# Regrouping a transposed activation in 4 KB rows: eight neighbouring feature blocks for each quarter of the partitions

## The chip, the cores and the metric

The kernel runs on one core of one Trainium2 chip. The metric is the device time of one execution in microseconds (us), as the median of repeated runs. Everything is float32.

## The reference

Two layers follow each other. The first is a global filter network: a real Fourier transform over the 3136 positions of each of 8 sequences, a product with a complex filter, and the inverse transform. The second is a feed-forward layer over the 25088 resulting rows, with 1024 hidden features:

```
X = rfft(x, axis=1);  y = irfft(X * (filt_r + 1j * filt_i))        # x: 8 x 3136 x 256
h = y.reshape(25088, 256) @ w_in                                    # 1024 features
solu = h * softmax(h)                                               # along the features
ln = (solu - mean(solu)) / sqrt(var(solu) + 1e-6) * g_ln
out = ln @ w_out                                                    # 1024 -> 256
```

## The kernel before

**Stages.** The Fourier transforms are written as matrix products with tables. A first stage (up to about 115 us) transforms sequence 0 alone and loads and converts the weights, which arrive as 64-bit words and are turned into float32 on VectorE, ScalarE and GpSimd (`load_words`, `load_float64`, `convert`). Then a loop over 196 steps `k` runs. One step handles 128 rows of the feed-forward layer; two steps make a pair `j`. Both matrix products of the layer use a seven-product scheme on a pair of row blocks, so operands have to be summed first: `pair_sums` for the first product (tiles `s`) and `project_sums` for the second (tiles `u`, and `solu_t` itself once), all on GpSimd through `sum_of` (L658). The transforms of sequences 1 to 7 are spread over the same steps by a table of step numbers (`PLAN`); they are done by about 1310 us.

**Order.** The order of all instructions on each engine is written out by hand in `step(k)`, under a manual schedule. Every engine runs its own queue in that order, and SyncE (SP) issues most transfers in that order too.

**The path of one block of rows.** `product` (L680, TensorE) makes `h` in PSUM; `keep` (L690, ScalarE) and `finish` (L701 and L704, VectorE) move it out and take the maximum; `exponential` (L712, ScalarE) and `normalize` (L723 to L728 on VectorE, L730 on ScalarE) give `solu` and its variance. The second product contracts over the features, so they have to come onto the partitions. `turn` (L738, VectorE) transposes 32 x 32 blocks of `solu` within each group of 32 partitions; four row blocks share one tile `turn`, laid out as [128 partitions, 32 feature blocks, 4 row blocks, 32]. `regroup` (L750) then moves the rest of the way by DMA, from SBUF to SBUF, on SP's queue: for each of two row groups of a pair it issues four transfers of 128 KB, one for each quarter `q` of the destination's partitions:

```
turned = turns[g].rearrange("p (k q) b i -> p k q (b i)", q=4)
for q in range(4):
    nc.sync.dma_start(out=st[32 * q:32 * q + 32, :, :],
                      in_=turned[32 * a:32 * a + 32, :, q, :])
```

Feature block `f` of 32 features is `f = 4 k + q` here: quarter `q` takes every fourth block, so a source row is eight separate pieces of 4 x 32 numbers, 512 B each, and the destination row is 4 KB in one piece. `solu_t` has two buffers for each row group, so a regrouping waits until the second product of two pairs before has read the buffer. After it, `project_sums` (L658, GpSimd) makes the sums, `project` (L792, TensorE) multiplies with `w_out_sb`, `keep_out` (L804, ScalarE) and `finish_out` (L809 and L811, VectorE) move the result out, and `store_out` (L819, SP) stores it. The small transfers `rows<-rs` (L758) and `rs_t<-rows` (L764) carry the reciprocal deviations from rows to partitions, on SP as well.

**The weights that follow this order.** `w_out_sb` and `g_sb` hold the features in the same order as `solu_t`. Four pieces of `w_out` (two halves of the features by two halves of the outputs) are each loaded by one GpSimd-issued transfer of 512 KB (L369), `(k p) d w -> p k d w`; `g_sb` comes by one transfer of single numbers (L536).

Of the kernel before, what the change touches and what calls it, by code (L numbers as in the profile page):

```python
# [17 lines left out]
P = 128  # L18
# [12 lines left out]
KD, KF = C // P, DFF // P  # L31
# [61 lines left out]
def kernel(  # L93
# [10 lines left out]
    nc = tc.nc  # L104
# [26 lines left out]
    g_sb = consts.tile([P, KF], FP32, name="g_sb")  # L131
# [11 lines left out]
    def words(ap):  # L143
        rows, cols = ap.shape
        return bass.AP(tensor=bass.DRamTensorHandle(ap.tensor.name, (2 * rows * cols,), I32),
                       offset=0, ap=[[2 * cols, rows], [2, cols], [1, 2]])

    w_in_words, w_out_words = words(moe_w_in), words(moe_w_out)
# [211 lines left out]
    with ExitStack() as st:  # L360
# [5 lines left out]

        def load_words(src, n):
            raw = wpool.tile([P, 512, 2], I32, name=f"raw_{n}", tag="raw")
            nc.gpsimd.dma_start(  # L369
                out=raw.rearrange("p (k d) w -> p k d w", d=src.shape[-2]) if len(src.shape) == 4 else raw,  # L370
                in_=src)
            return raw

        def load_float64(dst, raw, negate, share):
# [62 lines left out]
        for h in range(2):  # L437
            for half in range(2):
                weights.append((w_out_sb[:, (0, 6, 1, 2)[2 * h + half]].rearrange("p k d -> p (k d)"),
                                w_out_words[512 * h:512 * h + 512, P * half:P * half + P].rearrange(  # L440
                                    "(k p) d w -> p k d w", p=P)))

        def resident(held):
            def find(sp, u):
# [8 lines left out]
        def begin(j):  # L453
            raws[j] = load_words(weights[j][1], j)
# [35 lines left out]
        def idle(out):  # L490

            nc.tensor.matmul(out=out, lhsT=tables[0][0][:, 0, 0].rearrange("p u q -> p (u q)"),
                             rhs=filters[0][0][:, 0], start=True, stop=True)
# [13 lines left out]
        def start(i):  # L507
            sp.fetch_filter(i)
            sp.fetch_de(i)
            sp.forward(i, halves(f"pb_0_{i}"))  # L510
# [4 lines left out]
        for n in range(16):  # L515
            (nc.sync, nc.scalar)[n % 2].dma_start(
                out=t2_0[NH * (n % 4):NH * (n % 4) + NH, n // 4, :], in_=rows_x[n:n + 1])
# [6 lines left out]
        for i in range(units):  # L524
            if i + 2 < units:
                start(i + 2)
            sp.multiply(i, 0, nc.vector.tensor_tensor)
            sp.multiply(i, 1, nc.gpsimd.tensor_tensor)
            pss = [ps_t.tile([P, 2, C], FP32, name=f"pc_0_{i}_{u}", tag="t") for u in range(2)]
            idle(pss[0])  # L530
            sp.inverse(i, pss)
            sp.store(i, nc.scalar.dma_start)
            if i == 0:
                nc.gpsimd.dma_start(out=wi_t, in_=wi_dram)
                nc.gpsimd.dma_start(out=wq_t, in_=wq_dram)
                nc.gpsimd.dma_start(out=g_sb, in_=moe_g_ln.rearrange("(k p) -> p k", p=P))  # L536
            elif i != 2:
                begin({1: 2, 3: 3, 4: 4, 5: 5, 6: 6}[i])
        idle_row(14, "idler")
# [6 lines left out]
        for i0, n, rows in ((0, 4, P), (4, 4, P), (8, NP - 9, P), (NP - 1, 1, NQ)):  # L546
            f, at = filters[i0]
            nc.sync.dma_start(
                out=f_dram[i0:i0 + n].rearrange("i u q k c -> (u q) i (k c)")[0:rows],
                in_=f[0:rows, at:at + n].rearrange("p i k c -> p i (k c)"))  # L550
# [85 lines left out]
    def load_de(sp, u):  # L636
# [6 lines left out]
    turns, variances, solu_ts, solu_sums, rs_rows, rss, pos, ots = (  # L643
        {} for _ in range(8))
# [96 lines left out]
    def regroup(p, i):  # L741


        g, second = divmod(p, 2)
        turned = turns[g].rearrange("p (k q) b i -> p k q (b i)", q=4)
        a = 2 * second + i
        st = upool.tile([P, KF, P], FP32, name=f"solu_t_{p}_{i}", tag=f"solu_t{i}")
        solu_ts[p, i] = st[:, 0:KF // 2, :], st[:, KF // 2:KF, :]
        for q in range(4):
            nc.sync.dma_start(out=st[32 * q:32 * q + 32, :, :],  # L750
                              in_=turned[32 * a:32 * a + 32, :, q, :])
        if not second and i == 0:
            rs = small.tile([P, 4], FP32, name=f"rs_{g}", tag="rs", bufs=2)
            nc.gpsimd.tensor_scalar(out=rs, in0=variances.pop(g), scalar1=1.0 / DFF, scalar2=EPS_LN,
                                    op0=ALU.mult, op1=ALU.add)
            nc.gpsimd.tensor_tensor(out=rs, in0=rs, in1=neg_half, op=ALU.pow)
            rs_rows[g] = rows = rs_dram.tile([P, 4], FP32, name=f"rows_{g}", tag="rows")
            nc.sync.dma_start(out=rows, in_=rs)  # L758
# [137 lines left out]
    def step(k):  # L896
# [24 lines left out]
        if not odd and 0 <= j - 3 < pairs:  # L921
            regroup(j - 3, 0)
# [13 lines left out]
        if not odd:  # L936
            if hid:
                product(j, 6)
                keep(j, k + 1, 0)
            if proj:  # L940
                project(p, 3)
                project(p, 4)
            if 0 <= j - 3 < pairs:
                regroup(j - 3, 1)
            if 0 <= j - 4 < pairs:
                project_sums(j - 4, 1)
            if hid:
                product(j, 7)
        else:
            if proj:  # L950
                project(p, 1)
                keep_out(p, 0, (0, 0))
                project(p, 2)
                finish_out(p, 0, 0, (0, 0), 1)
            if hid:
                product(j, 3)
                product(j, 4)
            if 0 <= j - 3 < pairs:
                project_sums(j - 3, 0)
                if (j - 3) % 2 == 0:  # L960
                    regroup_deviations((j - 3) // 2)
            if proj:
                project(p, 6)
                project(p, 7)
# [52 lines left out]
```

## Time and profile before

| | |
|---|---|
| median of 6 runs | 1684.87 us (1677.85 to 1687.3) |
| the profiled execution | 1686.34 us, span 1684.6 us |
| granted TensorE clock, mean of the span | 0.986 |
| TensorE (PE) busy | 1602.5 us, 95% |
| VectorE (DVE), GpSimd (POOL), ScalarE (ACT) busy | 75%, 67%, 56% |
| bytes moved by DMA | 311.72 MB in 375957 packets |
| SP's queue (q1) | 306260 packets, 169.81 MB, 38.6% of the time of 16 DMA engines |
| `solu_t<-turn` (L750) | 784 transfers of 128 KB |

The page of the profile names engines as in the table; PEld is the loading of weights into TensorE, which overlaps the products, and SPq is SP's queue. A group of instructions is written as line, engine, operation, output tile `<-` input tiles, shape, count, then busy time and the mean of one, then the idle time of the engine just before these instructions and who ended it. Matrix products are pipelined and their ends are modelled, so a TensorE that is shown as busy need not run at its peak. All windows are in us from the start of the span.

### The profile page before, as it was taken

How to read it: one execution, taken by the hardware profiler on the slowest of the kernel's cores; microseconds unless marked ns; L12 is line 12 of the kernel's file. 1: busy time of each engine (PE TensorE's matmuls, PEld its weight loads, DVE VectorE, ACT ScalarE, POOL GpSimd, SP SyncE). 2: the span in 40 equal slices, each digit the busy share in tenths (PEclk: the TensorE clock that was granted, in tenths of full speed). 3: DMA queues.
4: the chain of work that ended last, by engine and by line, in shares of the span. 5: the costliest groups of instructions: out<-in, count | busy, mean ns of one | idle time of the engine just before them, and what ended most of it. 6: DMA issues, size and time to landing. Idle time of an engine off the chain costs nothing.

```text
span 1684.6 us, 31072 instructions
## 1 busy us (share of the span) xinstructions
PE 1602.5 (95%) x10022; PEld 1096.5 (65%) x10022; DVE 1265.9 (75%) x2619; ACT 937.9 (56%) x1730; POOL 1125.6 (67%) x1268
## 2 busy tenths in 40 slices
PE   5798899999999999999999999999999999999996
PEld 1353456756766676667766676667776777777776
DVE  1676787777778878887778878787778776777772
ACT  2154455556665555556565665556565566656551
POOL 4444777578666756687577866677566756676664
PEclk8998899999999999999999999999999999999999
DMA  9886868876788668865786658766775444444443
GB/s 260 248 276 208 238 182 230 215 200 181 195 240 226 179 180 232 222 188 149 210 241 197 176 152 234 226 183 167 200 210 166 114 124 123 100 108 107 110 110 94
DMA packets 375957, 311.72 MB, mean 185 GB/s; under 512 B 61514, under 2 KB 341571, under 8 KB 375795
## 3 DMA queue, kind: packets, MB, share of 16 engines
q1 hardware_dynamic: 306260, 169.81, 38.6%
q0 software_dynamic: 32640, 101.65, 20.2%
q10 hardware_dynamic: 36896, 38.28, 8.0%
q8 instruction: 81, 1.33, 0.3%
q14 instruction: 80, 0.66, 0.1%
HBM read 124.83 MB, written 81.50 MB: 122 GB/s over the span
## 4 chain that ended last, share of the span: by engine, by line
PE 65%; DMA 15%; DVE 8%; POOL 4%; issue 3%; SPq 3%; ACT 2%; ACTq 0%; DVEq 0%; POOLq 0%
PE m L680 27%; PE o L792 25%; DMA solu_t<-turn 7%; PE py L353 5%; SPq L750 2%; DMA x<-in_x_dram 2%; PE pb L292 2%; PE pc L292 2%; PE pa L260 2%; DVE h L728 2%; PE pa L217 2%; DMA t<-d 1%; DVE turn L738 1%; DMA rows<-rs 1%; DMA out_dram<-ot 1%
## 5 line engine op out<-in xcount | busy, mean ns | idle before, releaser
L730 ACT ACTIVATE e<-h,nmu 128x1024 f32<-128x1024 f32 x196 | 225.3, 1149 | 365.4 <-DVE h L728 363.5
L792 PEld LDWEIGHTS o<-w_out_sb,solu_t 128*128 128x128 f32 x3136 | 381.0, 192 | 61.0 <-issue 40.7
L792 PE MATMUL o<-w_out_sb,solu_t 128*128 128x128 f32 x3136 | 401.2, 276 | 12.1 <-DVE rsum L723 9.0
L680 PE MATMUL m<-w_in_sb,s 128*128 128x512 f32 x784 | 401.8, 604 | 4.3 <-ACT h L690 2.2
L792 PEld LDWEIGHTS o<-w_out_sb,u 128*128 128x128 f32 x2352 | 305.3, 192 | 146.9 <-issue 110.8
L658 POOL TENSOR_TENSOR u<-solu_t 128x512 f32<-128x512 f32 x98 | 146.1, 1491 | 307.1 <-DMA solu_t<-turn 178.1
L680 PE MATMUL m<-w_in_sb,y 128*128 128x512 f32 x588 | 316.0, 621 | 13.7 <-DVE nmax L704 10.5
L792 PE MATMUL o<-w_out_sb,u 128*128 128x128 f32 x2352 | 313.4, 276 | 6.3 <-ACT ot L804 4.6
L728 DVE SCALAR_TENSOR_TENSOR h<-e,rsum,h 128x1024 f32<-128x1024 f32 x196 | 292.2, 1491 | 6.9
L811 DVE SCALAR_TENSOR_TENSOR ot<-o,rs_t,ot 128x128 f32<-128x128 f32 x294 | 102.5, 348 | 204.7 <-ACT ot L804 168.7
L690 ACT COPY h<-m 128x512 f32<-128x512 f32 x294 | 173.7, 591 | 130.4 <-PE m L680 113.9
L738 DVE STREAM_TRANSPOSE turn<-h 128x1024 f32<-128x1024 f32 x196 | 242.3, 1236 | 0.8
L712 ACT ACTIVATE e<-h,nmax 128x1024 f32<-128x1024 f32 x196 | 226.3, 1155 | 0.0
L658 POOL TENSOR_TENSOR u<-solu_t,u 128x512 f32<-128x512 f32 x98 | 143.0, 1459 | 87.9 <-PE o L792 83.9
L704 DVE CUSTOM_DVE_ANT_0 h<-m,h 128x512 f32<-128x512 f32 x196 | 133.1, 679 | 83.4 <-ACT h L690 59.7
L680 PEld LDWEIGHTS m<-w_in_sb,y 128*128 128x128 f32 x588 | 95.7, 193 | 123.3 <-DVE nmax L704 64.6
L356 ACT COPY y<-py 128x392 f32<-128x392 f32 x128 | 109.5, 855 | 106.4 <-PE py L353 104.7
L353 PEld LDWEIGHTS py<-wi_t,t 100*128 100x128 f32 x1024 | 132.3, 192 | 54.0 <-issue 40.2
L680 PEld LDWEIGHTS m<-w_in_sb,s 128*128 128x128 f32 x784 | 123.9, 191 | 65.8 <-issue 45.6
L658 POOL TENSOR_TENSOR solu_t<-solu_t,solu_t 128x512 f32<-128x512 f32 x98 | 152.0, 1551 | 7.7
L658 POOL TENSOR_TENSOR u<-u,solu_t 128x512 f32<-128x512 f32 x98 | 136.9, 1397 | 0.7
L353 PE MATMUL py<-wi_t,t 100*128 100x98 f32 x1024 | 131.6, 273 | 0.8 <-DMA t<-d 0.4
(108 smaller groups left out, 1984.4 us busy)
## 6 DMA issues: line engine op xcount, KB each, us to landing
solu_t<-turn SPq DMA_DIRECT2D x784, 128.0 KB
out_dram<-ot SPq DMA_DIRECT2D x196, 128.0 KB
t<-d POOLq DMA_DIRECT2D x56, 400.0 KB, 4.9
d<-x POOLq DMA_DIRECT2D x100, 200.0 KB, 5.2
f<-f_dram POOLq DMA_DIRECT2D x39, 512.0 KB, 6.7
d<-g POOLq DMA_DIRECT2D x39, 512.0 KB, 5.1
t<-d ACTq DMA_DIRECT2D x36, 512.0 KB
x<-in_x_dram SPq DMA_DIRECT2D x112, 98.0 KB
```

Source lines behind the costliest of these rows:

```text
L353: nc.tensor.matmul(out=psv[:, i:2 * NCH - i:2 * NCH - 1 - 2 * i, :], lhsT=t4s[e, ch][:, i, cb * P:cb * P + P], rhs=wi_t, start=True, stop= ...
L356: evac(out=y[:, cb, t0:t0 + S].rearrange("p (r m j) -> p m j r", m=N2 // NCH, j=NCH)[:, ch:last + 1 - ch:last - 2 * ch], in_=psv.rearrange ...
L658: nc.gpsimd.tensor_tensor(out=out, in0=in0, in1=in1, op=op)
L680: nc.tensor.matmul(out=ms[j, bank], lhsT=lhsT, rhs=w_in_sb[:, w, :], start=m in (1, 2, 7), stop=True, skip_group_check=True)
L690: nc.scalar.copy(out=h_half(k, i), in_=ms[j, 0])
L704: nc.vector.tensor_tensor_reduce(out=h_half(k, i), in0=ms[j, bank], in1=h_half(*kept), scale=1.0, scalar=sofar, op0=ALU.add, op1=ALU.min, ...
L712: nc.scalar.activation(out=e, in_=hs[k], func=AFT.Exp, bias=nmaxs.pop(k)[:, 1:2], scale=-1.0, accum_out=esum)
L728: nc.vector.scalar_tensor_tensor(out=solu, in0=e, scalar=rsum, in1=solu, op0=ALU.mult, op1=ALU.mult, accum_out=nmu)
L730: nc.scalar.activation(out=e, in_=solu, func=AFT.Square, bias=nmu, scale=-float(DFF), accum_out=variances[g][:, i:i + 1])
L738: nc.vector.transpose(out=turns[g][:, :, i, :], in_=solus.pop(k).rearrange("p (f j) -> p f j", j=32))
L792: nc.tensor.matmul(out=pos[p, bank], lhsT=lhs[:, f, :], rhs=w[:, f, :], start=f == 0 and m in (1, 2, 7), stop=True, skip_group_check=True)
L811: nc.vector.scalar_tensor_tensor(out=ot, in0=pos[p, bank], scalar=rs, in1=out_half(p, *kept)[0], op0=ALU.mult, op1=ALU.add)
```

## The change

The order of the features on the partitions changes. Feature block `f` becomes `f = 8 q + k`: quarter `q` takes eight neighbouring blocks. A source row of a regrouping is then 8 x 4 x 32 numbers in one piece, 4 KB, like the destination row. The number of transfers (784), their size (128 KB) and their partitions stay. `w_out_sb` and `g_sb` are loaded in the new order; as the 128 partitions no longer follow from one regular step in memory, each of the four pieces of `w_out` and `g_sb` is loaded by four transfers of 32 partitions instead of one of 128. The order of instructions on the engines is otherwise the same: on GpSimd 15 more transfers are issued in the first stage, and no other instruction moves.

```
         def load_words(src, n):
             raw = wpool.tile([P, 512, 2], I32, name=f"raw_{n}", tag="raw")
-            nc.gpsimd.dma_start(
-                out=raw.rearrange("p (k d) w -> p k d w", d=src.shape[-2]) if len(src.shape) == 4 else raw,
-                in_=src)
+            if len(src.shape) == 3:
+                nc.gpsimd.dma_start(out=raw, in_=src)
+            else:
+                for q in range(4):
+                    nc.gpsimd.dma_start(
+                        out=raw[32 * q:32 * q + 32].rearrange("p (k d) w -> p k d w", k=KF // 2),
+                        in_=src[q])
             return raw
...
                 weights.append((w_out_sb[:, (0, 6, 1, 2)[2 * h + half]].rearrange("p k d -> p (k d)"),
-                                w_out_words[512 * h:512 * h + 512, P * half:P * half + P].rearrange(
-                                    "(k p) d w -> p k d w", p=P)))
+                                w_out_words.rearrange("(q h k p) d w -> h q p k d w", q=4, h=2, p=32)[
+                                    h, :, :, :, P * half:P * half + P]))
...
-                nc.gpsimd.dma_start(out=g_sb, in_=moe_g_ln.rearrange("(k p) -> p k", p=P))
+                for q in range(4):
+                    nc.gpsimd.dma_start(out=g_sb[32 * q:32 * q + 32],
+                                        in_=moe_g_ln.rearrange("(q k p) -> q p k", q=4, p=32)[q])
...
-        turned = turns[g].rearrange("p (k q) b i -> p k q (b i)", q=4)
+        turned = turns[g].rearrange("p (q k) b i -> p q k (b i)", q=4)
...
             nc.sync.dma_start(out=st[32 * q:32 * q + 32, :, :],
-                              in_=turned[32 * a:32 * a + 32, :, q, :])
+                              in_=turned[32 * a:32 * a + 32, q])
```

## The prediction

> **What bounds the kernel now.** I read the busy table and the slices first, then the DMA queues, then the stages, then who waits for whom, and the end last.
>
> ```profile
> PE 1602.5 (95%) x10022; PEld 1096.5 (65%) x10022; DVE 1265.9 (75%) x2619; ACT 937.9 (56%) x1730; POOL 1125.6 (67%) x1268
> PE   5798899999999999999999999999999999999996
> DMA  9886868876788668865786658766775444444443
> q1 hardware_dynamic: 306260, 169.81, 38.6%
> q0 software_dynamic: 32640, 101.65, 20.2%
> ```
>
> TensorE is busy in nearly every slice after the fifth; DMA is heavily used until about 1310 us and half as much after it. The change works on DMA, in SP's queue q1. So the question is how much of TensorE's remaining idle time hangs on those transfers. Busy time by stage (the transforms of sequences 1 to 7 end near 1310):
>
> ```profile
> core 0: us, PE busy (x) PEld busy (x) DVE busy (x) ACT busy (x) POOL busy (x), PEclk, DMA share, GB/s
> 168.00:210.00 42.00, 35.11 (x192) 16.49 (x191) 32.23 (x57) 18.91 (x36) 32.30 (x35) 0.88 0.80 236
> 210.00:1310.00 1100.00, 1078.20 (x7089) 748.54 (x7088) 875.83 (x1792) 649.30 (x1215) 774.40 (x879) 1.00 0.72 199
> 1310.00:1640.00 330.00, 328.22 (x1919) 241.35 (x1917) 249.08 (x562) 201.26 (x373) 220.45 (x235) 1.00 0.45 113
> 1640.00:1684.60 44.60, 30.79 (x241) 29.05 (x240) 13.07 (x29) 9.41 (x21) 19.37 (x16) 0.95 0.37 97
> ```
>
> From 210 to 1310 TensorE is idle for 1100 - 1078.2 = 21.8 us, from 1310 to 1640 for 1.8 us, and at the end for 13.8 us. These small numbers cap the change. Who waits, from 210 to 1310:
>
> ```profile
> POOL u L658 <- DMA solu_t<-turn: 155.5, 38, 7.7
> ...
> PE o L792 <- DVE rsum L723: 7.6, 20, 1.8
> PE m L680 <- DVE nmax L704: 7.0, 12, 1.1
> PE pa L260 <- POOL x L251: 3.9, 3, 1.6
> PE m L680 <- DVE h L701: 0.7, 3, 0.3
> ```
>
> GpSimd waits 155.5 us, 4.1 us at a time, for the regrouped tile. TensorE waits for VectorE (7.6 + 7.0 + 0.7 = 15.3 us) and a little for GpSimd (3.9 us), and hardly for a DMA. The chain of waits gives `solu_t<-turn` 7% of the span, but at two of its places that I looked at (517 and 553 us) the instruction named as released, L811, had stood in a VectorE queue with no idle time ahead of it. I take the 7% as no measure of a gain.
>
> **Part 1, the data movement.** 784 transfers of 256 pieces are 200,704 packets of 512 B; in the trace's packet records they take 32 ns each on the mean, which is 200,704 x 32 / 16 = 401 us for each of the 16 engines, 23.8% of the span. The change makes 784 x 32 = 25,088 packets of 4096 B. No SBUF to SBUF packet of that size is in the trace. The nearest rows are 4096 B packets of other transfers: 159 ns (median on q0 and q10), 218 ns (mean on q0 from 210 to 1310) and 241 ns (mean of the 1510 on q1, most of them in the crowded first stage). That bounds the new time at 249 to 378 us; I take 200 ns between the undisturbed and the crowded rows, 314 us, 18.6% of the span. DMA is relieved by about 5 points of its 72%.
>
> The rows of sizes give 512 B in 32 ns, 1024 B in 46 and 4096 B in 159, so 16, 22 and 26 bytes per ns: here small pieces between SBUF and SBUF do cost. The Trainium skill speaks against this change: "DMA: Bandwidth & Descriptors", section "Why small descriptors are slow (HBM only)", says that SBUF to SBUF transfers do not suffer the penalty of small descriptors. By that rule the packets would take as long as before in total, this term would be zero, and the sum would shrink to what the issue and the end give.
>
> **Part 2, the issue on SP.** L750 is 622 ns at the median, and 0.77 us on the mean from 168 to 1310 (425.5 us for 552). `rs_t<-rows` (L764) also goes to 32 partitions, each in one piece, and takes 424 ns (302 at least). I expect about 0.42 us, bounds 0.30 to 0.62. Four issues then save 4 x 0.2 = 0.8 us before the last of a group leaves.
>
> **Part 3, when GpSimd gets the tile.** Counting 256 packets to a transfer, the last packet ends 2.0 us after the issue from 1310 on, and 3.5 us (median; 6 at the ninth tenth) before it. A transfer's own share of an engine falls from 16 x 32 = 512 ns to 2 x 200 = 400 ns. With the issue (0.8), this (0.1) and, in the crowded stage, a shorter queue in front (1 us, two thirds of the 1.5 us by which the crowded landing exceeds the quiet one), a wait of 4.1 us shrinks by about 1.9 us: 38 x 1.9 = 72 of 155.5 us, 46%. That is GpSimd time, and most of it is covered: the sums made from the tile are read by TensorE one to two steps (6 to 12 us) later.
>
> **Part 4, what of it reaches TensorE between 210 and 1310.** Two ways are visible. First the direct wait for the sum L251, which stands behind the waiting sums in GpSimd's queue: 46% of 3.9 is 1.8 us (bounds 0 to 3.9). Second the meeting of GpSimd with VectorE:
>
> ```profile
> L728 DVE SCALAR_TENSOR_TENSOR h<-e,rsum,h 128x1024 f32<-128x1024 f32 x135 | 204.6, 1516 | 4.7
> ...
> L728 DVE SCALAR_TENSOR_TENSOR h<-e,rsum,h 128x1024 f32<-128x1024 f32 x51 | 71.1, 1395 | 1.8
> ```
>
> The first row is 210 to 1310, the second 1310 to 1640, where the tile lands early: L728 takes 1516 against 1395 ns; its shortest is 1283. It is longer where a GpSimd sum runs at the same time. VectorE's excess over 1283 is 135 x 0.233 = 31.5 us in the first stage, and TensorE's 15.3 us of waiting for VectorE make 0.49 us of each. If earlier landing brings L728 half way to the later stage's mean, 135 x 0.060 x 0.49 = 4.0 us are gained. Bounds: 15.4 us gained if all excess went; the loss is priced in the second rival. Part 4 is 5.8 us.
>
> From 168 to 210 I take nothing: TensorE's longest wait there (3.0 us) is for GpSimd's L315, behind a GpSimd queue that never waits for `solu_t`. From 1310 to 1640 nothing either, 1.8 us at most.
>
> **Part 5, the end.** After the last row block nothing covers the regrouping:
>
> ```profile
> 1660.92 6.31 SPq L750 DMA_DIRECT2D solu_t<-turn  x8
> 1669.18 1.27 POOL L658 TENSOR_TENSOR u<-solu_t 128x512 f32<-128x512 f32 x1 [4.66 <-DMA solu_t<-turn]
> 1673.15 1.13 PE L792 MATMUL o<-w_out_sb,u 128*128 128x128 f32 x8 [1.65 <-POOL u L658]
> ```
>
> Eight issues, the landing, three sums, then TensorE, which has waited 1.65 us. Eight faster issues (1.6 us) and 0.1 to 0.3 us of landing bring all of this forward by 1.7 us or more; then TensorE's own queue is next, so 1.65 us is the whole gain. If the issue stays at 0.62 us, 0.1 to 0.3 us is left.
>
> **Part 6, the extra loads.** GpSimd's issue of one `w_out` piece (512 runs of 1 KB) takes 0.78 us, of a `w_in` piece (128 runs) 0.58, of `g_sb` 0.93. Four of 128 runs each are 4 x 0.58 = 2.3, so 1.5 us more for each piece; `g_sb` becomes 4 x 0.6 = 2.4, likewise 1.5 more.
>
> - Behind `g_sb` stands the sum L315 of unit 1 (starts at 56.94): it would end near 59.7, and TensorE reads it at 63.97. Covered by 4 us.
> - Behind the `w_out` pieces at 73.49 and 76.65 stand the sums of units 5 and 6. The last one would start at 79.3 instead of 77.79 and end at 80.0, where TensorE wanted it at 79.56: TensorE and its row of idle products move by 0.5 us. At the price of 0.78 an issue it would be 1.4 us.
> - That shift meets a pause of 1.93 us at 117.5, where TensorE waits for a GpSimd sum that follows VectorE's conversions; these run without a gap from 77.6 to 112. So it costs nothing, and 0.5 to 1.4 us if that pause were not there.
> - The conversions need the pieces 8 us or more after they land, so the later landing is hidden.
>
> **The sum.** 0 + 5.8 + 0 + 1.65 = 7.4 us. Against the profiled execution, 1686.3 - 7.4 = 1678.9; that run is 1.5 us above the median of six, so against the median 1684.87 - 7.4 = 1677.5 us, 0.44% faster. What a measurement of this kernel can tell from no change is about 0.3%, 5 us. The forecast's own range is 1664 (all excess of L728, all 3.9 us and 1.65 gone: 21 us) to 1681.
>
> **Rivals.** First, the waits are covered: GpSimd's 155.5 us lie beside a busy TensorE, VectorE stays where it is, and only the end gains: 1684.9 - 1.65 = 1683.2. For it speak TensorE's 98% from 210 on and the absence of direct waits for DMA. Against it, the idle time is concentrated in the stage with crowded DMA.
>
> Second, slower: GpSimd takes the tile sooner and then holds up VectorE. The sum `u<-solu_t` has a median of 2.09 us from 1310 on and 1.27 before, so in the quiet stage it is GpSimd that loses 0.81 us to VectorE. If it starts 1.9 us sooner it can be ahead of L728, and VectorE loses this instead. With half of the 68 pairs between 210 and 1310, 34 x 0.81 x 0.49 = 13.5 us, minus the end: 1684.9 + 13.5 - 1.65 = 1696.7. It outweighs the other gains (1.65 + 1.8) once L728's mean there rises by 3.45 / 0.49 / 135 = 0.05 us, above 1.57 us. The same may come from L315 and L245, which meet GpSimd too.
>
> Third, the change does not do what it says: rows of 4 KB are cut to 512 B again, the packet count stays near 376 thousand, and the time stays at 1685.
>
> **Chances.** Forecast 0.50 (0.43 faster, 0.07 same); covered 0.24 (0.05, 0.16, and 0.03 slower); GpSimd ahead of VectorE 0.22 (0.02 same, 0.20 slower); rows cut 0.04 (0.03 same, 0.01 slower). That makes faster 0.48, same 0.28, slower 0.24. The range takes in the first rival and most of the second, 1664 to 1695.
>
> **What would show it.** Right: about 200 thousand packets, those of 4096 B on q1 at 160 to 240 ns; DMA share near 0.66 from 210 to 1310 and near 0.38 from there to 1640; L750 near 0.42 us; GpSimd's wait for `solu_t` near 85 us in that stage; L728 at 1.40 to 1.50 us; no wait of TensorE for `u` at the end. Wrong: L728 above 1.57 us, L750 still at 0.62, or GpSimd's waits gone while TensorE's idle time stays near 22 us.

## The result and the profile after

The changed kernel takes 1692.96 us, median of 24 runs (1684.81 to 1699.62), beside 1685.23 us for the kernel before, median of 48 runs (1677.82 to 1692.36). The ratio is 1.0044, 95% interval [1.0033, 1.0056]: 7.7 us slower, where 7.4 us faster was forecast. The profiled execution of the changed kernel took 1689.39 us, span 1687.6. Lines have moved by 6: the softmax product L728 is now L734, the sums L658 are L664, the regrouping L750 is L756.

From the page of the changed kernel, the busy table, the slices and the two large queues (packets, MB, share of 16 engines):

```profile
PE 1605.2 (95%) x10022; PEld 1098.4 (65%) x10022; DVE 1268.5 (75%) x2619; ACT 937.5 (56%) x1730; POOL 1127.9 (67%) x1283
...
PE   5898899999999999999999999999999999999997
...
DMA  9986868776788668766776668766785455444443
...
q1 hardware_dynamic: 130644, 169.81, 38.8%
q0 software_dynamic: 32928, 101.65, 20.1%
```

The pieces were joined: q1 has 175,616 packets fewer, 200,704 of 512 B having become 25,088 of 4096 B. The third column of q1 did not fall with them: 38.6% before, 38.8% now. Busy time by stage, changed kernel:

```profile
core 0: us, PE busy (x) PEld busy (x) DVE busy (x) ACT busy (x) POOL busy (x), PEclk, DMA share, GB/s
...
168.00:210.00 42.00, 34.43 (x194) 16.24 (x191) 31.38 (x56) 18.62 (x35) 32.03 (x35) 0.88 0.81 238
210.00:1310.00 1100.00, 1081.37 (x7120) 753.17 (x7118) 872.40 (x1801) 650.83 (x1218) 773.49 (x882) 1.00 0.72 199
1310.00:1640.00 330.00, 324.44 (x1871) 235.96 (x1870) 251.75 (x549) 198.16 (x366) 213.65 (x230) 1.00 0.46 110
1640.00:1687.60 47.60, 33.11 (x260) 31.19 (x259) 16.67 (x36) 10.89 (x24) 21.81 (x17) 0.95 0.40 98
```

DMA share stands where it was in every stage. TensorE's idle time shrank by 3.2 us from 210 to 1310 (to 18.6) and grew by 3.8 from 1310 to 1640 (to 5.6), in the stage where the forecast expected nothing. A second view of the same thing, counted from the trace's own records: the 196 transposes of VectorE (L738, now L744) mark the steps of the layer. From transpose 0 to 136 the kernel before takes 1120.8 us and the changed one 1115.0; from 136 to 144, 55.5 and 57.4; from 144 to 195, 328.9 and **337.0**. So the last stage lost 8.1 us, about the whole difference of the medians. The spans of these two executions differ by 3.0 us only (1684.6 and 1687.6), since the 5.8 us that the transform stage was shorter in this pair, and 1.2 us at the end, stand against it.

The waits of the changed kernel, 210 to 1310 (total us, times, longest), then the softmax product, first from 210 to 1310 and then from 1310 to 1640 (busy us, mean ns of one, idle before):

```profile
POOL u L664 <- DMA solu_t<-turn: 144.4, 36, 7.8
...
PE m L686 <- DVE nmax L710: 6.6, 11, 1.5
PE o L798 <- DVE rsum L729: 6.4, 22, 1.7
...
PE m L686 <- DVE h L707: 1.9, 4, 0.9
PE pa L260 <- POOL x L251: 1.8, 2, 1.1
```

```profile
L734 DVE SCALAR_TENSOR_TENSOR h<-e,rsum,h 128x1024 f32<-128x1024 f32 x136 | 202.3, 1487 | 4.8
...
L734 DVE SCALAR_TENSOR_TENSOR h<-e,rsum,h 128x1024 f32<-128x1024 f32 x50 | 78.5, 1570 | 1.8
```

GpSimd still waits 144 us for the tile (155.5 before), TensorE for VectorE 14.9 us (15.3 before) and for GpSimd's L251 1.8 (3.9 before). The product became a little shorter in the first stage (1516 before) and longer in the second (1395 before). There TensorE now waits for the VectorE operation that follows the product, from 1310 to 1640, before and after:

```profile
PE m L680 <- DVE h L701: 1.4, 3, 0.5
```

```profile
PE m L686 <- DVE h L707: 5.6, 14, 0.5
```

One place in the last stage shows how. Timeline of the kernel before (start, duration, instruction):

```profile
1550.11 1.28 DVE L728 SCALAR_TENSOR_TENSOR h<-e,rsum,h 128x1024 f32<-128x1024 f32 x1
1550.18 2.34 POOL L658 TENSOR_TENSOR u<-solu_t 128x512 f32<-128x512 f32 x1 [1.84 <-DMA out_dram<-ot]
...
1551.32 0.75 DVE L701 TENSOR_SCALAR_CACHE_REDUCE h<-m,nmax 128x512 f32<-128x512 f32 x1
```

And the same step of the changed kernel:

```profile
1549.19 1.26 POOL L664 TENSOR_TENSOR u<-solu_t 128x512 f32<-128x512 f32 x1 [1.66 <-DMA out_dram<-ot]
...
1549.31 2.23 DVE L734 SCALAR_TENSOR_TENSOR h<-e,rsum,h 128x1024 f32<-128x1024 f32 x1
...
1550.54 2.14 POOL L664 TENSOR_TENSOR solu_t<-solu_t,solu_t 128x512 f32<-128x512 f32 x1
...
1551.47 0.74 DVE L707 TENSOR_SCALAR_CACHE_REDUCE h<-m,nmax 128x512 f32<-128x512 f32 x1
...
1552.27 1.12 PE L686 MATMUL m<-w_in_sb,y 128*128 128x512 f32 x2 [0.38 <-DVE h L707]
```

At both places the one that starts first runs at its own speed (1.28 or 1.26 us), and the other takes about 1 us more (2.34 or 2.23 us). Before, VectorE starts 70 ns ahead here and GpSimd loses. After, GpSimd starts 0.12 us ahead, L734 takes 2.23 us, and TensorE stands 0.38 us for what VectorE does next. Over the 14 odd steps from 168 on, GpSimd's first sum starts 84 ns *after* L728 in the median before, with L728 at 1369 ns on the mean, and 84 ns *before* L734 after, with L734 at 2060 ns. The profile puts the sum's wait down to `out_dram<-ot`, but the sum follows its own tile: in these 14 steps it starts 0.37 to 0.56 us after the last packet of its regrouping before, and 0.39 to 0.61 us after it in the changed kernel. So an earlier tile is an earlier sum.

The page "SBUF — State Buffer" of the Trainium skill, section "SBUF: two separate sides", describes a port pair that VectorE and GpSimd share as an exclusive lock, held for a whole instruction by the one that starts first, the other blocking fully. The two timelines agree with it to about 0.2 us: by such a lock the second one would take its own time and what is left of the first one's, 2.47 and 2.42 us as an estimate from the rows above, where 2.34 and 2.23 were measured.

The end of the changed kernel, timeline:

```profile
1665.07 5.34 SPq L756 DMA_DIRECT2D solu_t<-turn  x8
...
1674.92 1.27 POOL L664 TENSOR_TENSOR u<-u,solu_t 128x512 f32<-128x512 f32 x1
...
1676.24 1.16 PE L798 MATMUL o<-w_out_sb,u 128*128 128x128 f32 x8
```

The eight issues and TensorE's products there no longer carry the 1.65 us of waiting for the sum.

### The profile page after: what moved, and what is told of

Read it like the earlier page. It is cut to its first block, busy times and chain, and to the rows that moved or that the text cites. A ratio compares the mean times of both kernels' runs of the same rounds, so it can differ in the third digit from the quotient of the medians.

```text
span 1687.6 us, 31097 instructions
## 1 busy us (share of the span) xinstructions
PE 1605.2 (95%) x10022; PEld 1098.4 (65%) x10022; DVE 1268.5 (75%) x2619; ACT 937.5 (56%) x1730; POOL 1127.9 (67%) x1283
## 3 DMA queue, kind: packets, MB, share of 16 engines
q1 hardware_dynamic: 130644, 169.81, 38.8%
## 4 chain that ended last, share of the span: by engine, by line
PE 60%; DMA 18%; DVE 9%; POOL 4%; issue 3%; ACT 3%; SPq 3%; ACTq 0%; DVEq 0%; POOLq 0%
PE m L686 24%; PE o L798 23%; DMA solu_t<-turn 9%; PE py L353 5%; DMA x<-in_x_dram 3%; DVE h L734 3%; PE pa L260 2%; SPq L756 2%; PE pc L292 2%; PE pb L292 2%; ACT e L718 1%; PE pa L217 1%; DVE turn L744 1%; POOL u L664 1%; DVE diff L245 1%
## 5 line engine op out<-in xcount | busy, mean ns | idle before, releaser
L686 PE MATMUL m<-w_in_sb,s 128*128 128x512 f32 x784 | 403.0, 605 | 4.6 <-ACT h L696 2.3
L686 PE MATMUL m<-w_in_sb,y 128*128 128x512 f32 x588 | 315.9, 621 | 18.2 <-DVE nmax L710 10.1
L664 POOL TENSOR_TENSOR u<-solu_t 128x512 f32<-128x512 f32 x98 | 138.1, 1410 | 274.9 <-DMA solu_t<-turn 169.1
L734 DVE SCALAR_TENSOR_TENSOR h<-e,rsum,h 128x1024 f32<-128x1024 f32 x196 | 297.1, 1516 | 6.9
L744 DVE STREAM_TRANSPOSE turn<-h 128x1024 f32<-128x1024 f32 x196 | 242.2, 1236 | 1.2 <-DVE ot L817 0.4
L664 POOL TENSOR_TENSOR u<-solu_t,u 128x512 f32<-128x512 f32 x98 | 141.7, 1446 | 115.5 <-PE o L798 112.0
L686 PEld LDWEIGHTS m<-w_in_sb,y 128*128 128x128 f32 x588 | 95.7, 193 | 128.2 <-DVE nmax L710 62.8
L686 PEld LDWEIGHTS m<-w_in_sb,s 128*128 128x128 f32 x784 | 124.2, 191 | 66.2 <-issue 45.5
L664 POOL TENSOR_TENSOR solu_t<-solu_t,solu_t 128x512 f32<-128x512 f32 x98 | 156.9, 1601 | 7.7
L664 POOL TENSOR_TENSOR u<-u,solu_t 128x512 f32<-128x512 f32 x98 | 135.7, 1385 | 0.7
```

What stands on the lines that cost most here:

```text
L664: nc.gpsimd.tensor_tensor(out=out, in0=in0, in1=in1, op=op)
L686: nc.tensor.matmul(out=ms[j, bank], lhsT=lhsT, rhs=w_in_sb[:, w, :], start=m in (1, 2, 7), stop=True, skip_group_check=True)
L734: nc.vector.scalar_tensor_tensor(out=solu, in0=e, scalar=rsum, in1=solu, op0=ALU.mult, op1=ALU.mult, accum_out=nmu)
L744: nc.vector.transpose(out=turns[g][:, :, i, :], in_=solus.pop(k).rearrange("p (f j) -> p f j", j=32))
```

## The experiments

The theory after the first look: the whole loss is the start order in the last stage. Rivals: the new loads in the first stage, the 4 KB pieces by some way of their own, or the regrouping's timing, with GpSimd's sums only showing it. Eighteen runs follow. In the table, "late" is the time from transpose 144 to 195 in the profiled execution, "product" the mean of L728 or L734 in the odd steps 168 to 196, "lead" the median start of GpSimd's first sum against it (negative: GpSimd first). "Shifted" variants moved other tiles in memory too, which x10 takes up. The late time repeats well (337.0 and 337.8 in two profiles of the changed kernel). The transform stage does not: with the code of before it took 1114.9 to 1123.0 us from transpose 0 to 136 in four profiles.

| run | kernel and edit | median us | ratio to before | late us | product ns | lead ns |
|---|---|---|---|---|---|---|
| | before | 1685.2 | | 328.9 | 1369 | +84 |
| | after | 1693.0 | 1.0044 [1.0033, 1.0056] | 337.0 | 2060 | -84 |
| x1_cut | after, pieces of 512 B | 1687.9 | 1.0011 [0.9984, 1.0038] | 330.0 | 1494 | +88 |
| x5_before_pause | before, memset 128 wide | 1685.3 | 0.9998 [0.9975, 1.0022] | 329.8 | 1447 | +62 |
| x8_before_late_pause | before, memset 384 wide, late | 1684.8 | 1.0009 [0.9989, 1.0029] | 330.1 | 1310 | -198 |
| x13_before_two_small | before, two small operations, late | 1704.4 | 1.0112 [1.0080, 1.0143] | 343.8 | 2058 | -279 |
| x2_after_guard | after, guard, tiles shifted | 1690.7 | 1.0027 [1.0004, 1.0050] | 325.7 | 1285 | +1532 |
| x6_after_late_guard | after, late guard, shifted | 1691.5 | 1.0046 [1.0032, 1.0059] | 326.6 | 1284 | +1532 |
| x7_before_late_guard | before, late guard, shifted | 1709.6 | 1.0158 [1.0135, 1.0181] | 325.7 | 1284 | +1532 |
| x4_after_late | after, delay, shifted | 1700.5 | 1.0084 [1.0055, 1.0113] | 331.4 | 1549 | +118 |
| x9_after_late_only | after, late delay, shifted | 1695.8 | 1.0078 [1.0055, 1.0102] | 327.9 | 1437 | +732 |
| x10_before_shift64 | before, shift alone | 1714.9 | 1.0179 [1.0146, 1.0212] | 330.3 | 1358 | +496 |
| x11_after_guard_kept | after, late guard | 1680.6 | 0.9965 [0.9943, 0.9986] | 325.7 | 1284 | +1532 |
| x12_before_guard_kept | before, late guard | 1683.9 | 0.9987 [0.9967, 1.0007] | 325.7 | 1284 | +1532 |
| x14_after_late_kept | after, late delay | 1687.4 | 1.0007 [0.9993, 1.0021] | 329.6 | 1589 | +734 |
| x15_after_guard_512 | after, late guard, tiles 256 B on | 1680.0 | 0.9960 [0.9940, 0.9980] | 325.7 | 1284 | +1532 |
| x16_after_guard_all | after, guard everywhere | 1675.8 | 0.9934 [0.9914, 0.9954] | 325.7 | 1284 | +1532 |
| x17_after_again | after, second profile | 1695.4, one run | | 337.8 | 2186 | -81 |
| x18_before_guard_all | before, guard everywhere | 1675.0 | 0.9935 [0.9911, 0.9960] | 325.7 | 1284 | +1532 |
| x19_after_guard_all_again | as x16 | 1675.2 | 0.9939 [0.9914, 0.9964] | 325.6 | 1285 | +1532 |

### Piece size or loads: x1_cut

New order and new loads, but each source row is read backwards, so that it falls into eight pieces of 512 B; the weights are indexed to match.

```
-                              in_=turned[32 * a:32 * a + 32, q])
+                              in_=turned[32 * a:32 * a + 32, q, ::-1])
...
-            nc.tensor.matmul(out=pos[p, bank], lhsT=lhs[:, f, :], rhs=w[:, f, :],
+            nc.tensor.matmul(out=pos[p, bank], lhsT=lhs[:, f, :], rhs=w[:, KF // 2 - 1 - f, :],
```

> New block order and new weight loads, but each quarter's eight blocks are written in reverse, so a regrouped row is eight pieces of 512 B again (w_out and g_ln are read in the reversed order). Theory R (the tile arrives about 0.15 us sooner, so GpSimd's first sum of a pair starts ahead of VectorE's L728 and blocks it, mostly after 1310 us): the arrival goes back to that of before, GpSimd's sum starts after L728 in the odd steps, L728 from 1310 to 1640 at about 1.40 us, 1685 us. Theory S (4 KB packets hold up other transfers): also about 1685, but with no change of L728. Theory F (the extra loads of the first stage cost the time): it stays at 1693.

Packets of 512 B at 32.0 ns, issues at 620 ns, lead back at +88 ns, and late 330.0: the loss goes with the pieces' size, by way of the issue and the landing. The loads and the order of the features cost nothing that this can tell.

### Holding the order with a guard: x2, x6, x7

In odd steps GpSimd's first sum is moved behind the softmax product, by a small GpSimd operation that reads four numbers of what L734 wrote; x2 does it in all odd steps, x6 from step 144, and x7 from step 144 in the kernel before.

```
             if 0 <= j - 3 < pairs:
-                project_sums(j - 3, 0)
+                if k < 144:
+                    project_sums(j - 3, 0)
...
             normalize(k - 2)
+        if odd and k >= 144 and 0 <= j - 3 < pairs:
+            if k < blocks + 2:
+                guard = small.tile([P, 4], FP32, name="guard", tag="guard", bufs=2)
+                sum_of(guard, solus[k - 2][:, 0:4], solus[k - 2][:, 0:4], ALU.add)
+            project_sums(j - 3, 0)
```

> The changed kernel; in odd steps GpSimd first reads four numbers of the block that L728 has just written and only then makes the first two sums of the pair, so they can't start ahead of the odd step's L728. Theory R: odd-step L728 goes to 1.29 us, and the time falls by the whole loss or more, to 1685 or below. Theories S and F: the sums only start later, nothing is gained, 1693 or slower.

> The changed kernel with the guard (GpSimd reads four numbers that the odd step's L728 has written, then makes the first two sums) from step 144 on alone, that is from about 1310 us on, where no transform runs. Theory R (L728 blocked by a sum that starts ahead of it, in the odd steps after 1310): odd-step L728 there at 1.285 us, the last stage some 8 to 10 us shorter than in the changed kernel, in all about 1684 us. Theory S (large packets hold up others, anywhere) or F (loads in the first stage): 1692 to 1694.

> The same late guard on the kernel before, whose odd-step L728 is blocked in 10 of 28 steps from 140 on. Theory R: about 3 to 4 us gained, 1681 to 1682 us. Theories S and F: 1685.

In all three the product fell to 1284 or 1285 ns and the late stage to 325.7 to 326.6 us, so the guard did what was asked. But the times rose or hardly fell, and x7 lost 26 us although its code differs only in the last stage: the time went in the transform stage, where nothing was touched. Its packets of 512 B took 36.5 ns, 32.0 before. That was no effect of the guard, as x10 shows below.

### Delaying GpSimd: x4, x9 and x14

One more GpSimd addition of 128x4 ahead of the first sum, about 0.2 us; in every odd step (x4), in those from step 144 on (x9), and the latter with the later tiles kept in place (x14).

```
             if 0 <= j - 3 < pairs:
+                if k >= 144:
+                    late_by = small.tile([P, 64], FP32, name="late_by", tag="late_by", bufs=2)[:, 0:4]
+                    sum_of(late_by, solu_ts[j - 3, 0][0][:, 0, 0:4], solu_ts[j - 3, 1][1][:, 0, 0:4], ALU.add)
                 project_sums(j - 3, 0)
```

> The changed kernel with one more small GpSimd instruction (4 numbers on 128 partitions, about 0.2 us) that reads the regrouped tile ahead of the first sum, so that this sum starts about 0.2 us later and nothing else moves. Theory R: the sum now starts after L728 from 1310 on, L728 there back at 1.35 to 1.45 us, about 1686 us: more work on GpSimd makes it faster. Theories S and F: 1693 or a little more.

> The changed kernel with the small GpSimd instruction of 0.2 us ahead of the first sum from step 144 on alone. Theory R: the sum starts after L728 there (it led by 0.08 us), odd-step L728 from step 168 on near 1.5 us instead of 2.06, and 5 to 8 us less than the changed kernel, 1685 to 1688. Theories S and F: 1693.

> The changed kernel with one GpSimd addition of 128x4 ahead of its first sum in odd steps from 144 (about 0.2 us, reading the same tiles), its tile 256 bytes wide so that no later tile changes its place modulo 512 bytes. Nothing else differs, the guard is not in it. Race theory: the first sum starts about 0.1 us after the softmax product in place of 0.08 ahead of it, L734 in odd steps of 168 to 196 goes from 2.06 to 1.3-1.5 us, turns 144 to 195 take 327 to 331 us in place of 337.0, packets 259 ns, and the time is 1683 to 1687. Rival (the guard gained by something else than the start order, such as moving all of GpSimd's sums): 1690 to 1694.

x4 and x9 carry the shift of the tiles and say nothing by their medians; late they took 331.4 and 327.9 us. x14 is free of it: 329.6 us late, within what was expected, and a ratio of 1.0007. The median is 0.4 us above its range, and the product at 1589 ns above its own, since 4 of 14 odd steps are still lost; in these the sum still starts between 26 ns ahead of the product and 34 ns after it. In 7 others the small addition itself came after the product's start and took 0.8 to 1.3 us, so that the sum started only after the product (hence a median lead of 734 ns). A small addition, which only adds work, takes the kernel back to the time of before: that speaks for the start order as the cause, and against some other thing that the guard does.

### Delaying VectorE in the kernel before: x5, x8, x13

The reverse: make the kernel before lose the race. x5 and x8 put a memset ahead of L728 in odd steps (128 wide; 384 wide and late), x13 two reciprocals of 128x1 in place.

```
+        if k % 2 and k >= 142:
+            nc.vector.reciprocal(out=rsum, in_=rsum)
+            nc.vector.reciprocal(out=rsum, in_=rsum)
```

> The kernel before with a VectorE memset of 128 numbers on 128 partitions (0.17 us) ahead of L728 in odd steps, so L728 comes 0.17 us later and GpSimd's sum, not moved, starts ahead of it. No DMA is changed. Theory R: L728 from 1310 on rises to about 1.6 us or more, and the time to about 1693, though VectorE has idle time for the 98 x 0.17 us. Theories S and F: 1685 to 1687.

> The kernel before with a VectorE memset of 384 numbers on 128 partitions ahead of L728 in odd steps from step 142 on, so that L728 starts 0.2 to 0.4 us later than GpSimd's sum; no DMA is changed. Theory R: odd-step L728 there at 1.8 us or more and the time up by 5 to 10 us, to 1690 to 1695. Theories S and F: 1685 to 1686.

> The kernel before, with two more reciprocals of 128x1 in place on rsum (each undoes the other) ahead of the softmax product at L728, in odd steps from 142. They take about 0.18 us each and, one element wide, should not keep GpSimd from starting, as the memset of the last trial did. Race theory: L728 starts some 0.3 us later and GpSimd's first sum gets ahead of it (lead about -250 ns); L728 in odd steps of 168 to 196 goes from 1.37 to about 2.0 us, the late stage loses 6 to 11 us, and the time is 1690 to 1696, the changed kernel's loss without the change. Rival (the loss needs the changed order or packets): L728 stays near 1.3 us, at most 28 x 0.36 us = 10 us if all the added work lay on the path, and by the earlier pause only 1 to 3: 1684 to 1688.

x5 moved L728 against the sum by some 0.02 us only (lead 84 to 62 ns) and decides nothing. In x8 GpSimd's sum starts 198 ns ahead of L728 and yet L728 is short: in its timeline the memset starts 0.07 us ahead of the sum and the sum takes 2.51 us. So the delay did not put the product behind the sum, and the experiment failed; but it gives the price of a delay of about 0.3 us with the race won in 12 of 14 odd steps: 1.2 us late (the product itself took 1.16 us there in place of 1.28).

The stamps of all runs say where the race turns. Counted from the end of the last reciprocal ahead of the product, sums that start up to 82 ns after it hold the product up, and from 87 ns on they wait for it; of 182 clear meetings in the 20 profiles (sums that start from 100 ns ahead of that end to 400 ns after it, where one of the two runs at its own speed) only two, at 85 and 86 ns, lie the other way round. Without a memset that is about 50 ns after the product's own start. In x5 and x8, where a memset stands between, the point is the same (75 to 87 and 78 to 91 ns). Whether the memset itself held GpSimd off in x8, or the product's claim dates from the reciprocal, these runs don't tell apart.

x13 moves the last reciprocal itself, and has such a delay with the race lost. From 1310 to 1640, its product and TensorE's wait (before: 1.4 us, 3 times):

```profile
L731 DVE SCALAR_TENSOR_TENSOR h<-e,rsum,h 128x1024 f32<-128x1024 f32 x49 | 75.5, 1541 | 1.7
```

```profile
PE m L680 <- DVE h L701: 9.0, 14, 0.9
```

13 of 14 odd steps lose, the product takes 2058 ns as in the changed kernel, and the late stage takes 14.9 us more. The kernel before thus shows the changed kernel's loss without the change. The expected price was too low (1690 to 1696, measured 1704.4): the lost 0.69 us and the added 0.36 us of each odd step add up, and of their sum of 1.05 us TensorE lost 0.83 (9.95 us in the 12 odd steps between transposes 168 and 192).

### The address of the later tiles: x10, x15

The guard's and the delay's first form had added two buffers of 32 bytes to the pool of small tiles. All tiles laid out after it (turned tiles, `solu_t`, the spectrum's) moved from 256 to 320 bytes past a multiple of 512. x10 is the kernel before with such a move and nothing else:

```
     nc.vector.memset(neg_half, -0.5)
+    shift = small.tile([P, 16], FP32, name="shift", tag="shift", bufs=1)
+    nc.vector.memset(shift, 0.0)
```

> The kernel before with one tile of 16 numbers (64 bytes per partition) added to the pool of small tiles and written once at the start. No instruction of the loops is touched; the turned tiles, solu_t, the spectrum's tiles and the products that are laid out behind that pool move from 256 to 320 bytes past a multiple of 512. Four of the variants that ran so far (the guards and the small GpSimd operation) moved them by the same 64 bytes, through two buffers of 32 bytes, and their regrouping packets took longer (512 B: 36.5 ns in place of 32.0). Theory A (the address alone costs): packets of 512 B take about 36.5 ns, the SBUF-to-SBUF queue's share rises by a tenth and more, and the time is 10 to 30 us above before. Theory B (the slower packets came of the added GpSimd work): packets 32 ns, time within 0.3% of before.

The share of q1 in its page, 38.6% before, and its transform stage (DMA share in the last but one column, 0.72 before):

```profile
q1 hardware_dynamic: 306260, 169.81, 41.6%
```

```profile
210.00:1310.00 1100.00, 1060.73 (x6919) 734.98 (x6918) 859.30 (x1739) 633.10 (x1181) 754.94 (x861) 1.00 0.77 196
```

An unused tile of 64 bytes costs 28 us. Packets of 512 B took 36.6 ns on the mean in place of 32.0 (14% more); in the shifted variants of the changed kernel those of 4096 B took 264 to 265 in place of 259 (2%), and the median of 4096 B packets on q0 went from 159 to 165. x15 moves the tiles by 256 bytes:

> The changed kernel with the late guard, whose tile is 128 bytes wide, so that the later tiles move by 256 bytes: the turned tiles, solu_t and the spectrum's tiles then start at multiples of 512. If what costs at 64 bytes past is a start that is no multiple of 256: packets of 4096 B 259 ns, as with the wide guard, and 1680 within 0.3%. If a multiple of 512 is better still, by the same mechanism: 250 ns or less, the DMA share of the transform stage under 0.70, and 1665 to 1677. If the address acts otherwise: slower than 1685.

258 ns and 1680.0 us: the same as x11 (260 ns, 1680.6 us, in the next section). Tiles at multiples of 256 and of 512 bytes cost the same, tiles 64 bytes past a multiple of 256 cost more; other places were not run.

The Trainium skill, "DMA: Bandwidth & Descriptors", section "How a descriptor splits into AXI transactions", says that a descriptor which does not start at a multiple of 256 bytes fetches from the boundary below. An estimate from that page: 512 B from 64 past a boundary are 18 beats of 32 bytes for 16, 12.5% more, and 4096 B are 130 for 128, 1.6% more. The runs show 14% and 2%.

### The guard with the tiles in place: x11, x12, x16

The same guard with its tile 256 bytes wide (two buffers, 512 bytes: every later tile keeps its place modulo 512).

> The changed kernel with the late guard (from step 144 GpSimd reads four numbers of what the softmax product at L734 wrote, before its first sum, in odd steps), the guard's tile now 256 bytes wide, so that the later tiles stand where they stand in the changed kernel modulo 512 bytes. Race theory (the late stage loses because GpSimd's first sum starts just ahead of the softmax product and holds it): L734 in odd steps of 168 to 196 goes from 2.06 us to 1.28, packets of 4096 B take 259 ns as in the changed kernel, the late stage gives back 8 to 12 us, and the time is 1680 to 1686. Rival (the regrouping's other timing costs the late stage, GpSimd's sums being only where it shows): 1690 to 1693 though L734 is short. If the address has nothing to do with it: 1691.5 as with the first late guard.

> The kernel before with the same late guard and the same wide guard tile. Theory of the address: packets of 512 B take 32.0 ns, the transform stage stands as in before, and the guard's late gain of about 3 us is left: 1679 to 1683, in place of the 1709.6 with the narrow guard tile. Rival (the guard itself costs the transform stage): 1700 and more again.

> The changed kernel with the guard in every odd step, not from 144 alone, and the wide guard tile. In the transform stage (210 to 1310 us) some 20 of 70 odd steps have L734 over 1.5 us; if these lie on the path as those of the last stage do, the guard is worth up to 20 x 0.9 = 18 us more than the late one: 1665 to 1678. If that stage is set by other waits (its DMA share is 0.72, and the pair takes longer there), holding GpSimd back costs what it gains or more: 1679 to 1690.

The late guard takes the changed kernel from 1693.0 to 1680.6 us, 12 us, and its late stage gives back 11.3 (337.0 to 325.7). In the kernel before it gives 3.2 us late, which that kernel was losing to the same race now and then; its median is 2.8 us lower, by an interval that holds 1. From 1310 to 1640 in x11:

```profile
L734 DVE SCALAR_TENSOR_TENSOR h<-e,rsum,h 128x1024 f32<-128x1024 f32 x52 | 73.7, 1417 | 1.8
```

The mean is 1417 and not 1284 since the sums, now later, meet the product in the even steps: in 14 of the 26 even steps of the last stage it takes 1.57 to 2.2 us, where the changed kernel has 1.28 in all but the last. The late stage is shorter all the same. The guard in every odd step gives 4.8 us more (x16): of the 70 odd steps up to transpose 140, 7 have a product over 1.5 us, 17 in the changed kernel and 26 before. The expected 18 us priced each at 0.9 us, but most of them take 1.5 to 1.7 us: what they take over 1.28 us adds up to 7.5 us in x11 and to 3.2 in x16.

### Does the loss repeat, and what is the change worth alone: x17, x18, x19

> The changed kernel as it is, for a second profile. If the lost race is what its time consists of, it shows again: L734 in odd steps of 168 to 196 near 2.06 us, turns 144 to 195 near 337 us. If the first profile was a chance: near before's 328.9 us, with L734 near 1.4.

It repeats: 337.8 us late, 13 of 14 odd steps lost. From 1310 to 1640:

```profile
L734 DVE SCALAR_TENSOR_TENSOR h<-e,rsum,h 128x1024 f32<-128x1024 f32 x50 | 79.5, 1590 | 1.8
```

Then both orders with the guard everywhere, on one chip:

> The kernel before with the guard in every odd step and the wide guard tile. If all that the change moves is the start order: the same time as the changed kernel with this guard, 1674 to 1679. If the earlier arrival (issues of 0.59 in place of 0.62 us and 4 KB pieces) is worth something of its own once GpSimd can't get ahead: 1679 to 1684, as the two late guards (1683.9 and 1680.6) lay 3.3 us apart. If the guard loses in the transform stage with this order: above 1685.

> The changed kernel with the guard in every odd step once more, on the same chip as the kernel before with it. The first time gave a ratio of 0.9934; the same again is 0.991 to 0.995. If the first was partly the chip's: 0.995 to 0.998.

1675.0 us for the kernel before and 1675.2 for the changed one, ratios 0.9935 and 0.9939. With the start order held, the change is worth nothing that these medians can tell, either way; by their intervals that is to within some 6 us. In the last stage the guarded kernels of both orders take 147.14 us from transpose 168 to 192, 12.26 for each pair. The steps from transpose 136 to 144, 55.5 us before and 57.4 in both profiles of the changed kernel, take 55.0 in both. Both kernels beat the kernel before, by 0.65% and 0.61%.

## Why the prediction was wrong

**Part 1, the transfers: wrong, out of its bounds.** 4096 B between SBUF and SBUF take 259 ns on the mean (271 in the median, 280 from 1310 on), where 200 was taken and 159 to 241 were the rows. Eight packets of 32.0 ns are 256. The time of an engine is 25,088 x 259.5 / 16 = 407 us in place of 401, against bounds of 249 to 378. The step that failed is the choice of rows: the 26 bytes per ns came from transfers that have DRAM at one end, and the regrouping moved 16 bytes per ns with either size of piece. Whether the kind of the ends makes this, or the 32 partitions of each regrouping, no run separates. The rule of the Trainium skill that the prediction set against itself ("DMA: Bandwidth & Descriptors", "Why small descriptors are slow (HBM only)") held here: by it the prediction itself worked out that this term is zero.

**Part 2, the issue: mis-sized.** 589 ns in the median for 622, inside the bounds but far from the 0.42 us that was taken; `rs_t<-rows` was not a near row. Four issues save 0.13 us in place of 0.8.

**Part 3, the tile's arrival: followed the two above.** From 1310 on the last packet ends 1997 ns after its issue (2025 before). With the issues that is 0.16 us sooner, and the measured lead moved by 0.168. GpSimd's wait shrank to 144 us and not to about 84.

**Part 4, the transform stage: sign probably right, size about 3.6 of 5.8 us.** The product fell by 29 of the expected 60 ns, the wait for L251 by 2.1 us where 1.8 was said, and TensorE's idle time by 3.2. One pair of profiles says little here. From transpose 0 to 136, four profiles with the code of before in that stage (before, x8, x12, x13) took 1120.1 us on the mean (1114.9 to 1123.0) and five with the changed code (after, x11, x14, x15, x17) 1116.5 (1115.0 to 1117.9). x1_cut, with pieces of 512 B, took 1120.5. The ranges overlap, so this is likely and not shown. With the guard everywhere the stretch took 1115.3 us in the order of before (x18) and 1112.0 and 1111.5 in the changed one (x16, x19), again some 3.5 us.

**Part 4, 1310 to 1640, "nothing either, 1.8 us at most": the step that decides.** It bounded a gain by TensorE's idle time and gave no bound for a loss. The loss was 8.1 us. A full TensorE is no cover against a longer VectorE: the product lies on the way to its next products (L707, then L686), and with 0.69 us more in an odd step TensorE lost 6.4 us in the 12 odd steps between 168 and 192, 77% of 8.3. The prediction had read that GpSimd's sum takes 2.09 us there because it loses to VectorE; it did not ask by how much. The answer stood in the trace of before: the first sums start 84 ns after the product in the median, half of what even the small real shift is. By the turning point, about 50 ns after the product's start, the real margin was some 34 ns.

**Part 5, the end: as said, and too small to be seen.** The 1.65 us of waiting for the sum is gone, but from transpose 195 to the end the changed kernel took 33.9 and 35.5 us in its two profiles, the kernel before 35.1.

**Part 6, the loads: right within about 1 us.** Transpose 0 falls at 144.3 us in the first profile of both kernels, with GpSimd 7.8 us busier up to 168; over the same four and five profiles it falls at 144.3 and 145.2 on the mean.

**The rivals.** The second had the mechanism, GpSimd ahead of VectorE, at the wrong place and with the wrong point of decision: L734 stayed under 1.57 us from 210 to 1310 (1487), and the kernel got slower in the last stage, where the prediction put nothing. That its 1696.7 us lie within 4 us of the measured time is luck. Its rate, 0.49 of VectorE's excess, was 0.77 in the last stage. The first rival, that the waits are covered, gives about what x18 and x19 show once the start order is held. The third is out: the packets are 4096 B.

## What to carry to other kernels

Where two engines exclude each other, read who starts first and by how much, find from the lost and won meetings where the race turns, and set the margin against the time by which the change moves either: a shift of 0.16 us decided 8 us here, and an earlier arrival was the harm. A dependency that fixes the better order (one four-number operation of GpSimd in each odd step) was worth 11 us in the kernel before. When an experiment adds a tile, keep every later tile at its place modulo 256 bytes, or the address may be measured in place of the idea (28 us for 64 bytes here, nothing for 256).

## What was not expected of the hardware

Transfers between SBUF and SBUF moved 16 bytes per ns and engine at 512 and at 4096 B (32.0 and 259 ns). A shift of all later tiles by 64 bytes cost 28 us, 14% on packets of 512 B and 2% on those of 4096 B. The race between VectorE's product and GpSimd's sum turned about 85 ns after the end of the reciprocal ahead of the product, also where a memset 384 wide put the product itself 0.3 us later (x8).
